# A scheduled attention and softplus kernel: the order of all tasks taken from a list of ranks, and the scheduler's durations reset

## The chip, the cores and the metric

The kernel runs on one core of a Trainium2 chip. The metric is the device time of one execution in microseconds (us); lower is better. A core has five engines that run side by side, each working through its own queue of instructions in order: PE (TensorE, matrix multiplication), ACT (ScalarE), DVE (VectorE), POOL (GpSimd) and SP (SyncE, which here only issues DMA transfers). They wait for each other through semaphores.

## The reference

```python
# q, k, v: (8, 8, 576, 64) float32 = batch, heads, rows, head size
kv  = einsum('bhsd,bhse->bhde', k, v)
out = einsum('bhsd,bhde->bhse', q, kv)
rms = sqrt(mean(out * out, axis=-1, keepdims=True) + 1e-06)
x   = (out / rms * g_norm), as (4608, 512)        # batch*rows, heads*head size
h   = x @ w_in                                    # w_in  (512, 2048), float64
g   = maximum(h, 0) + log1p(exp(-abs(h)))         # softplus
result = g @ w_out                                # w_out (2048, 512), float64
```

## The kernel before

**Arithmetic.** Each float32 operand of the large products is split into three parts, so that every product is a sum of three matmuls in a fast float32 format. The parts are made by ACT (`high`, and the copies that scale) and by DVE (`low`, `less`). The weights come as 64-bit floats: DVE and ACT take them apart with some eight instructions for each 128 x 512 piece (`weight`, lines 423 to 464) and split them (`split_weight`, lines 499 to 529).

**Stages.** There are 36 tiles of 128 rows.
- Attention: `kv_of` multiplies k and v of a batch (PE line 696), `rows` makes one tile of x: `turn_q` (PE line 776), `out_rows` (PE line 720), square (ACT line 793), sum (DVE line 724), root (POOL lines 727 and 728), norm (DVE line 732), `turn_x` (PE line 738).
- Narrow steps, `step`: 64 of them, over 12 blocks of 384 rows and the first four to six of 16 pieces of the hidden width. A step is `mm1` (PE line 864, 12 matmuls of 384 columns), softplus and split (ACT lines 886 and 888, DVE lines 875 and 879), and three `mm2` (PE line 871, three matmuls of 512 columns each). `mm1` of a block's first step needs the split of all three tiles of its block (`split`, ACT line 640, DVE lines 643 and 646).
- Wide steps, `wide_step`: 48 of them, over blocks of 512 rows and pairs of pieces. Each has seven products of six matmuls of 256 columns (PE line 1066, a scheme that saves one product in eight), copies of partial sums in between (ACT lines 1108 and 1112, DVE line 1116), softplus and split, and eight `mm2` of three matmuls of 512 columns (PE line 1137).

**Who sets the order.** No loop does. The code makes some 3,800 tasks with `plan.add`: the engine, an estimate of its time in ns, a function that issues the instructions, the tasks it needs, a place `pos` in a rough order, and the buffers that it takes and gives back. `Plan.order` then plays the program through: it keeps for each engine the time at which it is free, takes the tasks that could begin within `SOON` = 150 ns of the earliest one, and among those the one with the lowest `pos`. At the end the tasks are issued in the order of their planned starts. So durations, landing times and `pos` decide nothing but the order of each engine's queue; what the chip then does is up to the semaphores. In the kernel before, `pos` comes from formulas with some 150 numbers (`P0` to `P7`).

**Fillers.** Where the plan sees the tensor engine idle for 400 ns or more before the seventh `mm1`, it puts in a multiplication of unit matrices whose result nobody reads (`warm`, PE line 1232). Once in the queue it is executed, whether the engine is idle there or not.

**Loads.** All on SP's queue, in the order of the plan. A load that has a `behind` is also held until a certain `mm1` is done.

Of the kernel before, what the change touches and what calls it, by code (L numbers as in the profile page):

```python
# [18 lines left out]
P = 128  # L19
# [4 lines left out]
E = 1.0 / RADIX  # L24

# [35 lines left out]
class Plan:  # L61
# [4 lines left out]
    HANDOVER = {"PE": 250, "ACT": 120, "DVE": 120, "POOL": 150, "SP": 0}  # L66
    READY = {"PE": 2500, "ACT": 2500, "DVE": 4000, "POOL": 2500, "SP": 700}
    SWITCH = {("all", "rows"): 90, ("all", "kv"): 90, ("rows", "all"): 250, ("kv", "all"): 250, ("rows", "kv"): 140, ("kv", "rows"): 140}
    TOGETHER, PATIENCE = 1, 0.0
    LANDING, FILLED = 3500, 60000  # L70
# [13 lines left out]
    def add(self, engine, ns, run, after=(), pos=0.0, take=(), give=(), size=0, behind=None, follows=None, kind="all"):  # L84
        pos, behind = round(pos, 4), None if behind is None else round(behind, 4)
        t = Task(engine, ns, run, [a for a in after if a is not None], pos, list(take), list(give), size)
        for s in t.give:
            s.readers += 1
        self.tasks.append(t)
        t.follows = follows  # L90
        t.behind = behind
        t.kind = kind
        return t

    def order(self):
# [5 lines left out]
        ready = {}  # L101
# [24 lines left out]
        dma_free = 1500  # L126
        last_read = {}
        kind = "all"
        done, left = [], len(self.tasks)
        while left:  # L130
            best = None
            for engine, tasks in ready.items():
                options = []
                for t in tasks:
                    at = max(engine_free[engine], t.ready)
                    if t.size:
                        at = max(at, dma_free - 2500)
                    for i, s in enumerate(t.take):
                        others = sum(u.ring == s.ring for u in t.take[:i])
                        if engine == "SP" and s.ring in ("m", "n"):  # L140
                            others += self.KEEP
                        if len(free[s.ring]) <= others:
                            break
                        at = max(at, sorted(free[s.ring])[sum(u.ring == s.ring for u in t.take[:i])][0])
                    else:
                        options.append((at, t))
                if not options:
                    continue
                first = min(at for at, _ in options)
                options = [(at, t) for at, t in options if at <= first + self.SOON]  # L150
                small = [o for o in options if engine == "PE" and o[1].kind != "all"]
                if small:
                    rest = [o for o in options if o[1].kind == "all"]
                    if kind != "all":
                        options = [o for o in small if o[1].kind == kind] or small
                    elif rest and len(small) < self.TOGETHER and (
                            min(o[1].pos for o in small) + self.PATIENCE > min(o[1].pos for o in rest)):
                        options = rest
                at, t = min(options, key=lambda o: (o[1].pos, o[0]))
                if engine == "PE" and self.spare and self.spare[-1].start is None:  # L160
                    ring, run, ns, _ = self.spare
                    begin = max(engine_free["PE"], self.BEGIN, min(free[ring])[0] if free[ring] else at)
                    if begin + ns <= at:
                        s = Slot(ring)
                        at, t = begin, Task("PE", ns, lambda s=s: run(s), [], None, [s], [s], 0)
                        t.kind = "all"
                        s.readers = 1
                if best is None or at < best[0]:
                    best = (at, t)
            if best is None:  # L170
                raise RuntimeError("the plan is stuck at " + str([(e, t.pos, [s.ring for s in t.take if not free[s.ring]]) for e, ts in ready.items() for t in ts][:20]))
            at, t = best
# [9 lines left out]
            if t.engine == "PE":  # L182
                t.ns += self.SWITCH.get((kind, t.kind), 0)
                kind = t.kind
            t.start = at
            engine_free[t.engine] = at + t.ns
            t.end = at + t.ns + self.HANDOVER[t.engine]
            if t.size:
                dma_free = max(dma_free, at + t.ns) + t.size
                t.end = dma_free + (self.LANDING if dma_free > self.FILLED else 2000)  # L190
# [16 lines left out]
def kernel(  # L207
# [206 lines left out]
    def weight(j, pos, fetch_pos, behind):  # L414
# [11 lines left out]
        f = add("SP", 450, fetch, (), fetch_pos, [raw], size=1800, behind=behind)  # L426
        if wide:
# [43 lines left out]
            over_done.append(add("ACT", 910, beyond, [d3], pos + (4 if c < 4 else 0), [], [sq]))  # L471
# [136 lines left out]
    def load_q(b):  # L608
# [13 lines left out]
        for a in range(4):  # L622
            for p in range(0, NP, 2):
                q_loads[b].append(add("SP", 500, lambda a=a, p=p: run(a, p), (), pos + 0.1 * (2 * a + p // 2),
                                      [q_slots[b]] if not (a or p) else [], [], 1095, behind=pos - 3.5,
                                      follows=q_loads[b][-1] if a or p else None))

    def split(t, x, ready, pos):
# [20 lines left out]
        a = add("ACT", 640, high, [ready] + ([] if i == 0 else [first_high[n]]), pos, [dst] if i == 0 else [])  # L649
# [17 lines left out]
    def kv_of(b):  # L667
# [7 lines left out]
        for p in range(NP + 1):  # L675
# [4 lines left out]
            def load(src, s, p=p, tail=tail, n=n, ks=ks):  # L680
                if tail:
# [6 lines left out]
                       650 if tail else 850, behind=pos - 5.5) for of_v, (src, s) in enumerate(((k, ks), (v, vs)))]  # L688
# [11 lines left out]
            last = add("PE", 470, run, lds + ([last] if b < 2 else []), pos + 0.5 * p, [bank] if p == 0 else [], [ks, vs], kind="kv",  # L700
# [3 lines left out]
        kv_ready[b] = [add("ACT", 400, lambda: nc.scalar.copy(kvs[b % 2], bank.tile), [last] + o_tasks.get(b - 2, []),  # L704
                           pos + 2.5, [], [bank])]

    def rows(t):
# [38 lines left out]
        for b, r0, n, s0 in parts(t):  # L746
# [32 lines left out]
            ld = add("SP", 900, load, (), pos - EARLY[7] + P7[20 + t], [q_s] if not at_qa or t == 0 else [], [], 1220 * n // P,  # L779
                     behind=pos - 3.5, follows=first_load[0] if t and at_qa else None)  # L780
            first_load.append(ld)
            a = add("PE", 440, turn_q, [ld], pos - 1, [tp], [q_s])
            turned.append(add("ACT", 590, lambda n=n, r0=r0, tp=tp: nc.scalar.copy(part_of_qT(n, r0), tp.tile[:, :, :n]),  # L783
# [5 lines left out]
        a = o_task = add("PE", 484, out_rows, turned + need, x_pos(t - second), [o], [qT], kind="rows", follows=rows_done.get(t - 1))  # L789
        rows_done[t] = a  # L790
        for pt in parts(t):
            o_tasks.setdefault(pt[0], []).append(a)
        a = add("ACT", 600, lambda: nc.scalar.activation(new(x, [P, H, D]).rearrange("s (a k) d -> s a (k d)", k=2), o.tile, func=AF.Square,
                                                              scale=D ** -0.5), [a], pos, [x])
        a = add("DVE", 690, reduce, [a], pos, [r])
        a = add("POOL", 2300, root, [a], pos)
        a = add("DVE", 700, norm, [a, o_task], pos, [], [o, r])
        if t < BY_PE:
            a = add("PE", 440, turn_x, [a], pos + 0.5, [xp], [x])
            if t < AT_ONCE:  # L800
                split(t, xp, a, pos + 0.5)
            a = add("ACT", 600, lambda: nc.scalar.copy(new(xg, [P, KD, P]), xp.tile), [a], pos + 1, [xg], [xp])
            x_there[t] = [add("SP", 450, lambda: nc.sync.dma_start(
                out=x_of(t), in_=xg.tile), [a], pos + 1, [], [xg], 1000)]
            return
# [21 lines left out]
        if i == g - 1:  # L827
            stores = [add("SP", 450, lambda a=a: store(a), turns, pos + 0.5, [], [xb], 820 if g > 1 else 490)
                      for a in range(P // BL)]
            for u in range(t - i, t + 1):  # L830
                x_there[u] = stores
# [6 lines left out]
    def x_again(t):  # L838
# [3 lines left out]
                 x_there[t], pos - EARLY[9], [xt], [], 1000, behind=first_step["block", t // TB] - 5)  # L842
# [6 lines left out]
    def step(s):  # L849
# [32 lines left out]
        a = add("PE", 2100, mm1, x_split[n] + factors_done[0, c] + [m for _, m in mm1s[-1:]] +  # L882
# [9 lines left out]
        for i in range(TB):  # L892
            a2 = add("PE", 700, lambda i=i: mm2(i), [a] + factors_done[1, c] + [mm2s.get(i)], s + 1.5,
# [19 lines left out]
    def leave(ph, t, bank, done, pos):  # L913
# [20 lines left out]
        if ph == LAST and BY_PE <= t < n_tiles - TB:  # L934
# [8 lines left out]
            add("SP", 1600, store, [a], pos, [], [ot], 750)  # L943
# [15 lines left out]
    def units_of(ph, n):  # L959
# [3 lines left out]
        for j, us in enumerate(GROUPS):  # L963
# [9 lines left out]
            def fetch(v, src, after, size, first=first, xl=xl, x_part=x_part, pos=pos, cols=None):  # L973
# [3 lines left out]
                t = add("SP", 350, run, after, pos - AHEAD, [] if first else [xl], [], size, behind=pos - 2 * AHEAD,  # L977
# [57 lines left out]
            a = add("ACT", 1070 if m > 1 else 600, high, lds, pos, [dst])  # L1035
# [8 lines left out]
    def wide_step(k):  # L1044
# [25 lines left out]
        def multiply(u, q, after, pos, take=(), follows=None):  # L1070
# [4 lines left out]
            return add("PE", 710, lambda: product(u, q), unit_done[ph, n, u] + forms_done[p][f] + list(after), pos, take, give,  # L1075
# [32 lines left out]
        c1 = add("ACT", 380, lambda: nc.scalar.copy(place(Y), place(X)), [a1, a5], b + 0.1)  # L1108
        c5 = add("ACT", 390, v_copy, [a5], b + 0.12, [gv])
        a6 = multiply(3, Y, [c1], b + LATE[0])  # L1110
        a2 = multiply(2, X, [c1, c5], b + LATE[0] + 0.02, follows=a6)
        c6 = add("ACT", 380, lambda: nc.scalar.copy(place(Z), place(Y)), [a6], b + 0.65)  # L1112
        x2 = add("ACT", 400, lambda: softplus(gt()[:, 0, :HW], place(X)), [a2], b + 0.7)
# [7 lines left out]
        x4 = add("ACT", 400, lambda: softplus(gt()[:, 1, :HW], place(Z)), [a4], b + 1.9, [], [ab])  # L1121
# [39 lines left out]
        for c in range(2):  # L1161
            for i in range(TW):
                slot_pos = b + PACE + MM2[TW * c + i]
                a2 = add("PE", 700, lambda c=c, i=i: mm2(c, i),
# [70 lines left out]
    plan.spare = ("h", warm, 400, mm1s[6][1])  # L1235
    for t in plan.order():
        t.run()
# [30 lines left out]
```

## Time and profile before

| | |
|---|---|
| median of 3 runs | 858.6 us (857.62 to 860.17) |
| the profiled execution | 858.19 us, of which the span from the first to the last instruction is 856.4 us |
| PE busy | 843.0 us, 98% of the span |
| DVE busy | 704.1 us, 82% |
| ACT busy | 520.6 us, 61% |
| POOL busy | 76.6 us, 9% |
| moved by DMA | 167.07 MB, mean 195 GB/s |

Busy time of PE is counted from a matmul's start to its modelled end, so consecutive matmuls overlap in it; how long one task holds the engine is read from start to start. The first `mm1` starts at 44.09 us, the narrow steps reach to about 355 us, and the last matmul ends at about 852.6 us.

### The profile page before, as it was taken

Reading aid. Unit: us, or ns where it says so; the run is one execution under the profiler, and the core shown is the slowest. Engines: PE = TensorE matmul, PEld = TensorE weight load, DVE = VectorE, ACT = ScalarE, POOL = GpSimd, SP = SyncE. Lnnn points to the kernel's source line nnn. Section 1 sums busy time; section 2 is a strip of 40 time slices with the busy share of each in tenths; the row PEclk is TensorE's granted clock in tenths of the full one; section 3 lists DMA queues with packets and bytes.
Section 4 is the critical chain, followed back from the end, with each engine's and each line's share of the span. In section 5 each row is a group of like instructions: output and inputs, shape, how many; then the busy total and the mean of one; then the engine's idle time right before and its main releaser. Section 6 shows DMA issues by size and latency. Waiting matters only on the chain.

```text
span 856.4 us, 17075 instructions
## 1 busy us (share of the span) xinstructions
PE 843.0 (98%) x6464; PEld 754.1 (88%) x6464; DVE 704.1 (82%) x995; ACT 520.6 (61%) x980; POOL 76.6 (9%) x79
## 2 busy tenths in 40 slices
PE   8899999999999999999999999999999999999998
PEld 5578898999898999999999999998999899999996
DVE  7888898888788889798898788878788766788873
ACT  6766665446344567766667665655868555566654
POOL 0351223111113300000000000000000000000000
PEclk9999999999999999999999999999999999999999
DMA  9998997778884755436644546645364753777864
GB/s 283 297 233 212 261 273 232 185 245 218 214 188 119 194 160 185 142 110 207 210 156 154 180 151 206 195 158 181 124 197 138 234 168 102 240 237 246 249 189 131
DMA packets 239778, 167.07 MB, mean 195 GB/s; under 512 B 106320, under 2 KB 198736, under 8 KB 239696
## 3 DMA queue, kind: packets, MB, share of 16 engines
q1 hardware_dynamic: 239392, 165.86, 65.9%
q8 instruction: 50, 0.82, 0.4%
q14 instruction: 32, 0.26, 0.1%
q10 hardware_dynamic: 304, 0.13, 0.1%
HBM read 112.98 MB, written 52.95 MB: 194 GB/s over the span
## 4 chain that ended last, share of the span: by engine, by line
PE 94%; ACT 1%; DVE 1%; DMA 1%; issue 1%; POOL 0%; SPq 0%; POOLq 0%; DVEq 0%; ACTq 0%
PE banks L1137 31%; PE banks L1066 28%; PE banks L871 16%; PE banks L864 15%; PE banks L720 2%; PE banks L696 2%; DMA loads<-in_k_dram 1%; PE banks L738 0%; PE banks L1232 0%; PE banks L776 0%; DVE units L643 0%; DVE half L732 0%; DVE roots L724 0%; POOL roots L728 0%; ACT w L783 0%
## 5 line engine op out<-in xcount | busy, mean ns | idle before, releaser
L1137 PE MATMUL banks<-pieces,gv 128*128 128x512 f32 x768 | 236.8, 390 | 0.0
L1137 PE MATMUL banks<-pieces,g_False 128*128 128x512 f32 x384 | 149.4, 389 | 0.0
L1137 PEld LDWEIGHTS banks<-pieces,gv 128*128 128x128 f32 x768 | 132.5, 188 | 17.2 <-DVE banks L910 0.2
L864 PE MATMUL banks<-units,pieces 128*128 128x384 f32 x768 | 144.8, 337 | 0.0
L871 PE MATMUL banks<-pieces,gv 128*128 128x512 f32 x576 | 143.3, 393 | 0.0
L864 PEld LDWEIGHTS banks<-units,pieces 128*128 128x128 f32 x768 | 134.7, 188 | 4.5
L871 PEld LDWEIGHTS banks<-pieces,gv 128*128 128x128 f32 x576 | 106.2, 188 | 19.0
L1066 PEld LDWEIGHTS banks<-units,pieces 128*128 128x128 f32 x840 | 111.0, 188 | 6.5 <-ACT banks L1112 0.4
L1066 PE MATMUL banks<-units,pieces 128*128 128x256 f32 x840 | 115.2, 280 | 0.0
L886 ACT ACTIVATE half<-banks 128x384 f32<-128x384 f32 x64 | 31.4, 491 | 94.0 <-PE banks L864 90.7
L1127 DVE TENSOR_TENSOR gv<-g_True,gv 128x1024 fp32r<-128x1024 f32 x47 | 57.5, 1223 | 35.6 <-ACT gv L1124 35.5
L1137 PEld LDWEIGHTS banks<-pieces,g_False 128*128 128x128 f32 x384 | 72.1, 188 | 15.0
L1066 PEld LDWEIGHTS banks<-units,w 128*128 128x128 f32 x504 | 66.7, 188 | 3.7 <-ACT banks L1112 0.2
L1066 PE MATMUL banks<-units,w 128*128 128x256 f32 x504 | 69.6, 280 | 0.0
L728 POOL TENSOR_TENSOR roots<-roots,half 128x8 f32<-128x8 f32 x36 | 62.3, 1731 | 3.0
L1130 DVE SCALAR_TENSOR_TENSOR g_False<-gv 128x1024 fp32r<-128x1024 f32 x47 | 57.6, 1225 | 1.5
L1029 DVE TENSOR_TENSOR units<-loads,units 128x1024 fp32r<-128x1024 f32 x42 | 51.2, 1219 | 6.0 <-ACT units L1026 5.9
L1094 ACT ACTIVATE g_True<-banks 128x256 f32<-128x256 f32 x96 | 36.7, 384 | 30.6 <-PE banks L1066 29.9
L1116 DVE TENSOR_TENSOR g_True<-banks,g_True 128x512 f32<-128x512 f32 x48 | 33.1, 690 | 25.8 <-PE banks L1066 19.8
L931 ACT ACTIVATE m<-banks 128x512 f32<-128x512 f32 x72 | 42.1, 595 | 18.2 <-PE banks L1137 12.5
L1032 DVE SCALAR_TENSOR_TENSOR units<-units 128x1024 fp32r<-128x1024 f32 x42 | 51.4, 1224 | 1.7
L1026 ACT ACTIVATE units<-loads 128x1024 fp32r<-128x1024 f32 x42 | 44.3, 1056 | 12.4 <-PE banks L1066 10.1
(115 smaller groups left out, 1248.7 us busy)
## 6 DMA issues: line engine op xcount, KB each, us to landing
loads<-x SPq DMA_DIRECT2D x180, 128.0 KB, 2.7
part<-m SPq DMA_DIRECT2D x72, 256.0 KB, 3.1
m<-part SPq DMA_DIRECT2D x72, 256.0 KB, 3.4
loads<-form SPq DMA_DIRECT2D x45, 256.0 KB, 3.2
form<-loads SPq DMA_DIRECT2D x36, 256.0 KB, 3.0
raw<-in_moe_w_in_dram SPq DMA_DIRECT2D x16, 512.0 KB, 4.7
loads<-in_k_dram SPq DMA_DIRECT2D x32, 256.0 KB, 4.0
loads<-in_v_dram SPq DMA_DIRECT2D x32, 256.0 KB, 4.5
```

The costliest lines, as they stand in the source:

```text
L728: nc.gpsimd.tensor_tensor(out=r.tile, in0=r.tile, in1=half, op=ALU.pow)
L864: nc.tensor.matmul(from_the_end(hp, w), lhsT=w_in.tile[:, i, kd * P:(kd + 1) * P], rhs=from_the_end(xv.tile[:, i, kd], w), start=(m == 0), ...
L871: nc.tensor.matmul(mine[i].tile, lhsT=gv.tile[:, m, i * P:(i + 1) * P], rhs=w_out.tile[:, m], start=(c == cs[0] and m == 0), stop=(c == cs ...
L931: a = add("ACT", 690 if ph == LAST else 600, lambda: nc.scalar.activation(new(ot, [P, d_model]), bank.tile, func=AF.Copy, scale=scale if p ...
L1026: nc.scalar.activation(part_of(0, F32R), xl.tile if m > 1 else xl.tile[:, 0], func=AF.Copy, scale=DOWN)
L1029: nc.vector.tensor_tensor(out=part_of(1, F32R), in0=xl.tile if m > 1 else xl.tile[:, 0], in1=part_of(0), op=ALU.subtract)
L1032: nc.vector.scalar_tensor_tensor(out=part_of(2, F32R), in0=part_of(1), scalar=-RADIX, in1=part_of(0), op0=ALU.mult, op1=ALU.add)
L1066: nc.tensor.matmul(from_the_end(place(q), (16, 8)[kd]), lhsT=w[:, m, at:at + P], rhs=from_the_end(dst.tile[:, m, v, kd] if u < 6 else dst. ...
L1094: nc.scalar.activation(dst, src, func=AF.Softplus, scale=1.0 + E)
L1127: nc.vector.tensor_tensor(out=gvt(1, F32R), in0=gt(), in1=gvt(0), op=ALU.subtract)
L1130: nc.vector.scalar_tensor_tensor(out=gt(F32R), in0=gvt(1), scalar=-RADIX, in1=gvt(0), op0=ALU.mult, op1=ALU.add)
L1137: nc.tensor.matmul(from_the_end(mine[i].tile, P), lhsT=(gvt(m, F32R) if m < 2 else gt(F32R))[:, c, i * P:(i + 1) * P], rhs=from_the_end(ou ...
```

## The change

Three things change; no task is added, taken away or altered.

1. The scheduler's estimates: tasks of ACT, DVE and POOL are taken shorter by a constant (`AHEAD`), hand-over times and several durations are reset, a change of the kind of matmul is priced differently, a load is priced by an entry time, its size and a fixed landing, and holds back later ones when too many descriptors or transfers are under way (`room`). Tasks on the PSUM rings `o` and `tp` wait until other engines have left the ring (`touched`).
2. After all tasks are made, each `pos` is overwritten by a number of the list `RANK`.
3. `Plan.order` runs as before with these, and lays in its fillers by its own reading.

```diff
+RANK = [
+    0, 7, 8, 9, 10, 12, 13, 14, 19, 22, 24, 28, 33, 38, 1, 16, 17, 21, 27, 30, 31, 34, 37, 42, 47, 51, 55, 61, 18, 44, 43, 45, 49, 53, 54, 57, 60, 64, 79,
...
+    3779, 3781, 3783, 3782, 3785, 3788, 3784, 3787, 3790, 3789, 3791, 3792, 3793, 3794,
+]
...
-    HANDOVER = {"PE": 250, "ACT": 120, "DVE": 120, "POOL": 150, "SP": 0}
-    READY = {"PE": 2500, "ACT": 2500, "DVE": 4000, "POOL": 2500, "SP": 700}
+    HANDOVER = {"PE": 205, "ACT": 140, "DVE": 121, "POOL": 145, "SP": 0}
+    AHEAD = {"PE": 0, "ACT": 107, "DVE": 88, "POOL": 110, "SP": 0}
+    READY = {"PE": 1600, "ACT": 3250, "DVE": 3050, "POOL": 2500, "SP": 700}
...
-    LANDING, FILLED = 3500, 60000
+    ENTRY, LANDING, DESCS, MOVES = 1770, 790, 2560, 8
...
-        t = Task(engine, ns, run, [a for a in after if a is not None], pos, list(take), list(give), size)
+        t = Task(engine, ns - self.AHEAD[engine], run, [a for a in after if a is not None], pos, list(take), list(give), size)
...
-                    at = max(engine_free[engine], t.ready)
-                    if t.size:
-                        at = max(at, dma_free - 2500)
+                    at = max([engine_free[engine], t.ready, *(end for b in t.banks for e, end in touched[b].items() if e != engine)])
...
+            if t.size:
+                at = room(t, at)
...
-                dma_free = max(dma_free, at + t.ns) + t.size
-                t.end = dma_free + (self.LANDING if dma_free > self.FILLED else 2000)
+                dma_free = max(dma_free, at + self.ENTRY) + t.size
+                t.end = dma_free + self.LANDING
...
-            return add("PE", 710, lambda: product(u, q), unit_done[ph, n, u] + forms_done[p][f] + list(after), pos, take, give,
+            return add("PE", 700, lambda: product(u, q), unit_done[ph, n, u] + forms_done[p][f] + list(after), pos, take, give,
...
+    assert len(RANK) == len(plan.tasks)
+    for t, at in zip(plan.tasks, RANK):
+        t.pos = at
     for t in plan.order():
         t.run()
```

`RANK` has 3,795 numbers, one for each task in the order in which the code makes them, and no number twice. Sorted by it, every task stands behind all that it needs, so the list can be read as one order of the whole program. For PE, up to the ninth `mm1`, with one letter for a task (M `mm1`, 2 `mm2`, k `kv_of`, r `out_rows`, q `turn_q`, x `turn_x`, l the two matmuls of a weight's split; fillers left out):

```
before      kkqlqlkkkqlrrqqkxlqqkrrxkqlxkkqrxrMxrlqxMkkrMxrl2x22222xM22kkk2rrMl22kkr2xMx222M222M222x22M
by RANK     qqlkkqlqqkkklrrlqqkkrxlqxrklkkxrrxMlMxM2rkkq2q22r22xMkkkr2xx2l2rM2M2xrkk2rM22M22x22x222M
```

## The prediction, made before the changed kernel was run

> **What bounds the kernel now.** I began with the windows view, which sets the engines side by side stage by stage.
>
> ```profile
> core 0: us, PE busy (x) PEld busy (x) DVE busy (x) ACT busy (x) POOL busy (x), PEclk, DMA share, GB/s
> 4.70:44.00 39.30, 32.72 (x458) 23.43 (x457) 35.33 (x60) 30.13 (x60) 9.55 (x11) 1.00 1.06 299
> 44.00:64.00 20.00, 18.68 (x214) 15.54 (x213) 17.35 (x31) 12.70 (x25) 9.80 (x9) 1.00 0.93 237
> 64.00:94.00 30.00, 29.89 (x306) 25.76 (x305) 26.40 (x46) 19.80 (x40) 6.44 (x6) 1.00 0.90 230
> 355.30:856.40 501.10, 497.33 (x3162) 450.96 (x3160) 399.11 (x470) 313.48 (x574) 0.00 (x0) 1.00 0.58 182
> ```
>
> From 64 us on PE has no gap to speak of; before that it has, while DVE is busy 90% of the time and the DMA engines all of it. So only the start can give much. What PE does there is seen in the groups by line and in the timeline:
>
> ```profile
> L1232 PE MATMUL banks<-ident_r 128*128 128x512 f32 x52 | 18.8, 480 | 2.0 <-DVE ident_r L1192 1.6 <-ACT pieces L529 0.2
> ```
>
> ```profile
> 42.59 1.66 PE L1232 MATMUL banks<-ident_r 128*128 128x512 f32 x6
> 44.09 2.25 PE L864 MATMUL banks<-units,pieces 128*128 128x384 f32 x12
> ```
>
> L1232 is the filler: 52 of them, 50 of these before the first `mm1` starts at 44.09 us. A busy PE is therefore not a useful PE, and I counted useful time instead. From start to start in the timeline, a task that follows its own kind takes: `mm1` 2.086 us, `mm2` 0.680, a product 0.700, a wide `mm2` 0.680. So 64 x 2.086 + 192 x 0.68 + 336 x 0.70 + 384 x 0.68 = 760.4 us; the small tasks (40 `kv_of` of 0.468, 36 `out_rows` of 0.515, 22 transposing tasks of about 0.38, 8 of 0.55 and a few more) add 50.7. Useful work W = 811.1 us of a span of 856.4: **45.3 us are lost**. With x the useful work that is done by a moment t, the loss so far is t - x:
>
> - first `mm1`: t 44.1, x 15.5, lost 28.6
> - fourth `mm1`: t 63.9, x 31.7, lost 32.2
> - ninth `mm1`: t 93.7, x 59.2, lost 34.5
> - end of the narrow steps: lost 40.5; wide steps: about 1 more; behind the last matmul, while the last tile is stored: 3.9.
>
> The ninth `mm1` opens the third block. Its DVE split ends at 92.9 us, 0.8 us before it starts, and the thirteenth likewise: DVE's queue sets the openings of blocks, up to about 115 us.
>
> **The change part by part.** No instruction is added, so W stays. I read `RANK` as an order (every task stands behind its needs), put in the durations above, and compared what stands ahead of what. Fillers, and swaps within 150 ns, I can't read from it.
>
> *To the first `mm1`.* 34 PE tasks ahead in both; on DVE 64 tasks ahead, before 62. Back to back, two DVE instructions of 0.69 us start 0.61 us apart (34.21 and 34.82 us), so +1.2 at most. Against it: the six fillers ahead of the first `mm1`, 1.5 us, may not stand there. I take 0; bounds -1.5 and +1.2.
>
> *First to ninth `mm1`.* In the new order the second and third `mm1` follow the first with one small task in between each (x 18.3 and 20.7, before 19.8 and 23.3). The last DVE instruction that the first `mm2` needs has 8 fewer DVE tasks ahead of it (70, before 78), 4.9 us. Splits of later tiles move back in exchange. The ninth `mm1` has the same DVE work ahead (73.1 us by the kernel's estimates less 88 ns each, before 73.4) but less useful PE work behind it: x 57.5, before 59.2. If DVE gets there no sooner, that is a loss of 1.7 - 0.3 = +1.4. But DVE idles: 39.3 - 35.33 + 20 - 17.35 + 30 - 26.40 = 10.2 us of the 89 before that point. The waits view says for what (ACT's squares, roots, PE's rows): neighbours in the queue that were not ready. That is what a better order takes away. With none of it regained +1.4; with all of it -8.8, but the changes of kind on PE (an `mm1` ahead of a `kv_of` takes 2.18 us instead of 2.09) can't go, about 1.6 of the 5.9 lost here, so -4.3 at the most. I take half, 1.4 - 5.1 = **-3.7**: the named waits of DVE from 44 to 116 us add to 6.9 us, so about half of the idle time belongs to neighbours that another order can exchange, and the rest to chains in which one DVE instruction feeds the next.
>
> *Rest of the narrow steps.* 6.0 us are lost here. In the whole order PE changes 75 times between `kv_of`, `out_rows` and the rest, before 70: 5 x 0.09 = +0.5. Between an `mm1` and the first `mm2` that needs it, beyond ACT's and DVE's time, lies a median of 7.2 us of PE work, before 3.0. That cushion covers waits of the kind that PE has at 77.5 us, where an `mm2` of 0.68 us holds it for 0.95. I take -1.1 for them, so **-0.6**; bounds -2 and +1.5.
>
> *Wide steps.* In the order before, 4 places have one product only between a product and the next that needs ACT's copy of it, 0.06 us more than copy and hand-overs take; PE lost 0.00, 0.07, 0.09 and 0.11 us at them. In the new order there are 27, and 5 wide `mm2` stand 0.1 us too early for their split. So 23 x 0.07 + 5 x 0.1 = +2.1; less the 1 us that the old stalls cost, which fall where the order is now another: **+1.1**; bounds -0.5 and, with 0.11 and late copies at each, +4.
>
> *Loads.* Their distance to their use, in PE work:
>
> ```profile
> DMA to landing us min/median/max: 2.1/2.8/5.2
> ```
>
> That is line 976, the wide steps' loads of x. The shortest PE work between such a load and the product it feeds, less ACT's and DVE's time, falls from 7.6 to 4.7 us; for the 72 loads of partial sums (median 3.4, longest 6.1) it stays 4.1. At the median nothing waits: 0, bounds 0 and +2, in the range. [...]
>
> *End.* The last `mm2` run is the same 15 tasks: 0.
>
> Sum: 0 - 3.7 - 0.6 + 1.1 + 0 = -3.2. The profiled execution took 858.19 us (1.8 around the span), 0.4 under the median of 858.6; so 855.0, or **855.4** for a median.
>
> **The rivals.**
> 1. *DVE's queue is as slow as before.* Then the ninth `mm1` comes at +1.4 and the sum is 0 + 1.4 - 0.6 + 1.1 = +1.9, with +1.2 ahead of the first `mm1` and +1.5 for the narrow steps +5.2: 860.5, up to 863.8. It ends slower, in DVE's queue ahead of the ninth and thirteenth `mm1`, and it decides from the point where DVE regains less than 1.4 us of idle time. For it: ahead of the fifth `mm1`, which opens block two, the new order has 55.5 us of DVE work, before 43.1. Against it: idle time with named waits is there to be had.
> 2. *The gain is given back in the wide steps.* All 27 tight places cost 0.11, loads land late, ACT's queue stands wrong: +4 there, so 858.6 - 3.7 - 0.6 + 4 = 858.3. For it: PE has no gap there now, so any disorder can only cost. Against it: some 28 old places with 0.44 us to spare cost nothing.
> 3. *DVE regains nearly all of it.* -4.3 - 1.5 - 2 + 0 = -7.8: 850.8.
> 4. *The clock falls.* The first 13 fillers start 0.43 us apart up to 6.9 us, later ones 0.23: PE ran at half speed there, though the row of the granted clock shows 1.00. If the new fillers leave a longer gap near 45 us, two `mm1` at half speed cost 2 x 2.09 = 4.2: 859.6. [...]
>
> That the change does nothing can be left out: of 1,085 PE tasks only 177 keep the same successor.
>
> **How the numbers follow.** Forecast 0.45, rivals in order 0.22, 0.18, 0.10, 0.05. The forecast's own range is 851 to 858. A measurement of this kernel can tell about 0.3%, 2.6 us: faster is under 856.0, slower over 861.2. Faster: 0.36 of the forecast and all of rival 3, 0.46. Within: 0.09 of the forecast, 0.05 of rival 1, 0.11 of rival 2, 0.02 of rival 4, 0.27. Slower: 0.17 of rival 1, 0.07 of rival 2, 0.03 of rival 4, 0.27. The range runs from rival 3's 850.5 to 863, close to rival 1's end.
>
> **What would show it.** Right: the first `mm1` within 1.5 us of 44.1; the fourth at a loss of about 30 (t near 60); the ninth before 90 us; DVE busy over 92% from 44 to 90; fewer than 45 fillers; the wide stage 0 to 2 us longer. Wrong: the ninth `mm1` at 92 us or later, a PE row in the waits view above 1 us past 100 us, or a wide stage over 4 us longer.

## The result, and the profile after

The changed kernel takes 865.52 us (median of six runs, 864.3 to 868.38) where the kernel before took 858.73 beside it: a ratio of 1.0086, 95% interval 1.0066 to 1.0106. It is slower by 6.8 us; the forecast was 3.2 us faster. The profiled execution took 865.74 us, its span is 864.0 (before 856.4).

The windows view of the changed kernel, over nearly the stretches that were shown of before (columns: stretch, length, then busy time and instructions of PE, PEld, DVE, ACT and POOL, granted clock, share of the DMA engines, GB/s):

```profile
4.70:44.00 39.30, 30.27 (x378) 21.87 (x376) 33.63 (x58) 28.66 (x57) 9.21 (x9) 0.87 0.98 271
44.00:64.00 20.00, 19.67 (x248) 16.61 (x247) 18.56 (x33) 12.85 (x27) 6.57 (x7) 1.00 0.98 246
64.00:94.00 30.00, 29.18 (x334) 25.26 (x333) 25.92 (x45) 21.17 (x43) 11.35 (x10) 1.00 0.99 259
356.00:864.00 508.00, 504.19 (x3177) 453.81 (x3175) 397.26 (x470) 311.91 (x575) 0.00 (x0) 1.00 0.57 180
```

Between 44 and 64 us DVE is indeed busier than before (18.56 us, was 17.35). But the first row has a granted clock of 0.87 where before had 1.00, and from 64 to 94 us PE is now the less busy one. The filler and the first `mm1`, in the groups by line and the timeline, and the loads of x in the view of their line:

```profile
L1401 PE MATMUL banks<-ident_r 128*128 128x512 f32 x42 | 15.4, 482 | 1.6 <-DVE ident_r L1361 1.6
```

```profile
46.73 2.36 PE L1033 MATMUL banks<-units,pieces 128*128 128x384 f32 x12
```

```profile
DMA to landing us min/median/max: 2.1/2.8/5.8
```

Ten fillers fewer, the first `mm1` 2.6 us later, and loads that land as before, at the median. (Lines of the changed kernel stand 169 further down: L864 is L1033, L1066 is L1235, L1112 is L1281.)

Where the 7.6 us of span went is seen with the prediction's own measure: t - x, the time that has passed less the useful PE work done by then. Each row is worked out from the starts of PE's tasks in one kernel's trace; the kernels below the second row are the experiments that follow.

| lost at x = | 0 | 15.6 (first `mm1`) | 30 | 60 | 110 | 320 | 810 |
|---|---|---|---|---|---|---|---|
| before | 8.4 | 28.6 | 32.2 | 34.5 | 36.9 | 40.6 | 41.6 |
| changed | 9.9 | 31.1 | 32.7 | 35.7 | 40.4 | 44.2 | 49.2 |
| clock_kept | 9.7 | 29.6 | 31.2 | 34.4 | 38.2 | 41.9 | 47.9 |
| wide_old_own | 9.8 | 28.7 | 30.3 | 34.7 | 39.3 | 42.7 | 43.6 |
| wide_new_own | 8.9 | 31.5 | 35.1 | 37.4 | 39.8 | 45.9 | 51.0 |
| after_short | 9.7 | 30.2 | 31.9 | 35.9 | 39.7 | 43.1 | 46.7 |
| before_short | 8.5 | 30.5 | 34.1 | 36.4 | 38.9 | 42.6 | 43.3 |
| after_split | 9.5 | 29.1 | 30.7 | 34.9 | 39.4 | 42.7 | 53.2 |
| before_split | 8.2 | 29.6 | 33.2 | 35.5 | 38.0 | 41.6 | 43.7 |
| start_new | 9.6 | 30.5 | 32.1 | 43.6 | 46.1 | 49.8 | 50.7 |
| start_old_own | 8.5 | 28.7 | 35.9 | 39.2 | 43.0 | 47.4 | 52.4 |
| narrow_new | 9.7 | 29.6 | 31.2 | 33.7 | 37.0 | 40.6 | 41.8 |
| narrow_new_clock | 9.6 | 27.4 | 29.0 | 31.8 | 35.5 | 39.2 | 40.2 |
| margin | 9.3 | 31.4 | 33.8 | 36.1 | 39.5 | 45.7 | 48.6 |
| margin_old_start | 8.4 | 28.1 | 31.0 | 33.3 | 37.7 | 43.3 | 44.7 |

Row by row, the changed kernel loses 2.4 us more than before up to the first `mm1`, wins 2.0 from there to x = 30 (the fourth `mm1`), and loses 0.8 to x = 60, 2.2 to x = 110, 0.2 to the end of the narrow steps and 3.9 in the wide steps: together the 7.6, but for rounding.

Two stretches can be read across kernels that have the same order there. From x = 15.6 to x = 30 the changed order loses 1.6 to 1.7 us and the old one 3.6, in every one of them. The first column that counts, x = 15.6, is not so sure: with the changed start and no added fillers it is 28.7 to 31.1, with the old start 28.1 to 31.5. So one execution differs from the next by some 3 us there, and most of the 2.4 us between the first two rows may be chance: over the six rows with each start the mean is 29.9 for the changed one and 29.5 for the old.

### The profile page after: what moved, and what is told of

Read it like the earlier page. It is cut to its first block, busy times and chain, and to the rows that moved or that the text cites. A ratio compares the mean times of both kernels' runs of the same rounds, so it can differ in the third digit from the quotient of the medians.

```text
span 864.0 us, 17031 instructions
## 1 busy us (share of the span) xinstructions
PE 847.4 (98%) x6454; PEld 753.9 (87%) x6454; DVE 697.6 (81%) x995; ACT 518.4 (60%) x980; POOL 79.2 (9%) x79
## 4 chain that ended last, share of the span: by engine, by line
PE 94%; DMA 3%; ACT 1%; DVE 1%; SPq 0%; issue 0%; DVEq 0%; ACTq 0%
PE banks L1306 30%; PE banks L1235 28%; PE banks L1040 15%; PE banks L1033 14%; PE banks L865 2%; PE banks L889 2%; DMA loads<-in_k_dram 1%; DMA early<-in_q_dram 1%; DMA raw<-in_moe_w_in_dram 1%; PE banks L1401 1%; PE banks L907 0%; PE banks L945 0%; DMA g<-in_k_dram 0%; SPq L854 0%; PE banks L694 0%
## 5 line engine op out<-in xcount | busy, mean ns | idle before, releaser
L1306 PE MATMUL banks<-pieces,gv 128*128 128x512 f32 x696 | 215.3, 391 | 0.0
L1040 PE MATMUL banks<-pieces,gv 128*128 128x512 f32 x576 | 147.8, 395 | 0.2 <-DVE gv L1048 0.2
L1033 PE MATMUL banks<-units,pieces 128*128 128x384 f32 x768 | 145.2, 337 | 0.1
L1033 PEld LDWEIGHTS banks<-units,pieces 128*128 128x128 f32 x768 | 134.6, 188 | 5.2 <-ACT half L1055 0.6
L1306 PE MATMUL banks<-pieces,g_False 128*128 128x512 f32 x348 | 135.6, 390 | 0.0
L1306 PEld LDWEIGHTS banks<-pieces,gv 128*128 128x128 f32 x696 | 119.6, 188 | 15.3
L1235 PEld LDWEIGHTS banks<-units,pieces 128*128 128x128 f32 x924 | 121.0, 188 | 8.5 <-ACT banks L1281 2.3
L1235 PE MATMUL banks<-units,pieces 128*128 128x256 f32 x924 | 127.6, 282 | 0.0
L1040 PEld LDWEIGHTS banks<-pieces,gv 128*128 128x128 f32 x576 | 105.3, 188 | 18.5 <-DVE gv L1048 0.7
L1306 PEld LDWEIGHTS banks<-pieces,g_False 128*128 128x128 f32 x348 | 65.3, 188 | 13.9
L1263 ACT ACTIVATE g_True<-banks 128x256 f32<-128x256 f32 x96 | 36.3, 379 | 42.6 <-PE banks L1235 41.9
L1235 PE MATMUL banks<-units,w 128*128 128x256 f32 x384 | 54.2, 281 | 0.0
L1235 PEld LDWEIGHTS banks<-units,w 128*128 128x128 f32 x384 | 51.3, 188 | 3.1 <-ACT g_True L1260 0.2
L1195 ACT ACTIVATE units<-loads 128x1024 fp32r<-128x1024 f32 x41 | 43.3, 1057 | 16.5 <-PE banks L1235 9.9
L1293 ACT ACTIVATE gv<-g_True 128x1024 fp32r<-128x1024 f32 x47 | 49.9, 1061 | 1.4
```

What stands on the lines that cost most here:

```text
L1033: nc.tensor.matmul(from_the_end(hp, w), lhsT=w_in.tile[:, i, kd * P:(kd + 1) * P], rhs=from_the_end(xv.tile[:, i, kd], w), start=(m == 0), ...
L1040: nc.tensor.matmul(mine[i].tile, lhsT=gv.tile[:, m, i * P:(i + 1) * P], rhs=w_out.tile[:, m], start=(c == cs[0] and m == 0), stop=(c == cs ...
L1195: nc.scalar.activation(part_of(0, F32R), xl.tile if m > 1 else xl.tile[:, 0], func=AF.Copy, scale=DOWN)
L1235: nc.tensor.matmul(from_the_end(place(q), (16, 8)[kd]), lhsT=w[:, m, at:at + P], rhs=from_the_end(dst.tile[:, m, v, kd] if u < 6 else dst. ...
L1293: nc.scalar.activation(gvt(0, F32R), gt(), func=AF.Copy, scale=DOWN)
L1306: nc.tensor.matmul(from_the_end(mine[i].tile, P), lhsT=(gvt(m, F32R) if m < 2 else gt(F32R))[:, c, i * P:(i + 1) * P], rhs=from_the_end(ou ...
```

## The experiments

Most of these kernels keep all instructions and change queues. Their edit is the same few lines: `Plan.order` no longer chooses, it follows a list of tasks (-1 is a filler) and a list of the buffers that each task had in the order it comes from. Each ratio is to the kernel before, run again beside that kernel (medians 858.4 to 859.8).

```diff
-        while left:
-            best = None
...
+        for item in ORD:
+            t = self.tasks[item]
...
+                for f in free[s.ring]:
+                    if n < len(wanted) and f[1] == wanted[n]:
+                        place = f
```

**Which stage.** The old order behind the changed narrow steps, and the changed order behind the old ones. In the first pair about 250 tasks got other buffers than in the order they come from, in the second pair, "own", only about ten.

> All engines' queues follow the new order up to the last narrow step (the first 1,620 of the 3,837 entries) and the old order from there on. Theory A (the wide steps lose 3.9 us in the new order because products stand too close to the copies they wait for): 865.5 - 3.9 = 861.6 us, PE from 356 us on as in the kernel before. Theory B (loads that come late and a cold start are the whole loss, the wide steps only pass it on): 864.5 to 865.5 us.

> The opposite: the old order up to the last narrow step, the new order for the wide steps. Theory A: 858.7 + 3.9 = 862.6 us, with some 37 stalls of 30 to 110 ns of PE behind 356 us. Theory B: 858.7 to 859.5 us.

> As wide_old (new order up to the last narrow step, old order from there), but each task takes the buffer that it had in the order it comes from, but for 12 tasks; in wide_old 252 tasks had another. Theory A (the order of the wide steps costs 3.9 us): the wide steps lose 1.0 us as in the kernel before, 865.5 - 3.9 = 861.6 us. Theory E (which buffer is taken counts as much as the order): wide_old's 863.2 us falls by the 1.4 us that its wide steps lost over those of before, to 861.8 us; if buffers do not count it stays at 863.2.

> As wide_new (old order up to the last narrow step, new order from there), with each task's own buffer but for 8 tasks; in wide_new 233 had another and the wide steps lost 10.8 us. Theory A: 858.9 + 3.9 = 862.8 us. Theory E: the same, and 5 us below wide_new's 867.9. If buffers do not count: 867.9 again.

Measured: 863.17 (ratio 1.0043, 1.0029 to 1.0057) and 867.92 (1.0100, 1.0085 to 1.0115); with their own buffers 859.60 (1.0015, 1.0004 to 1.0025) and 865.96 (1.0079, 1.0065 to 1.0093). Taking the changed wide order away brings back 5.9 of 6.8 us (by the two intervals, give or take some 2 us); putting it behind the old narrow steps costs 7.3, of which some 2.4 arise at the seam (6.1 us lost from x = 110 to 320, in before 3.7). Which buffer a task gets matters as well: 863.17 or 859.60 with one and the same order.

**The start.** Nine more fillers ahead of PE's first task, and nothing else changed; then the old order for the first 260 or 270 entries with the changed order behind it.

> The changed kernel with 9 more fillers ahead of the first task of PE, so that PE does not stand still from 6.05 to 9.90 us. Theory C (PE's half speed from 9.9 to 17.3 us delays the k and v products, these hold the four load buffers, and the loads start late): first mm1 at 45 us or before, 865.5 - 1.5 = 864.0 us or less. Theory D (the start is late because of the order of the loads alone): first mm1 at 46.5 us, 865.3 us or more.

> The old order up to the first mm1 (its first 260 entries, fillers included), the new order from there. Theory A': the first mm1 is back at 44.1 us instead of 46.7, and the narrow steps keep the whole of it: 865.5 - 2.4 = 863.1 us. Theory B': DVE's queue takes most of it back by the ninth mm1, as it did in the changed kernel (loss there 35.7, before 34.5): 864.5 to 865.5 us.

> Old order up to just behind the first mm1 (270 entries), new order from there, each task with its own buffer but for 6 tasks; in start_old 516 had another, and it took 875.2 us. Theory A' (the late start is kept to the end): 865.5 - 2.0 = 863.5 us. Theory B' (DVE's queue takes it back by the ninth mm1): 865 us. If buffers do not count: 875 us.

clock_kept took 863.41 (1.0051, 1.0039 to 1.0063), 2.1 us under the changed kernel; the same fillers were worth 1.9 us in each of two other orders further down. The timeline of PE in the changed kernel and the windows view of both, changed kernel first, show why:

```profile
3.90 2.15 PE L1401 MATMUL banks<-ident_r 128*128 128x512 f32 x7
9.90 1.09 PE L945 MATMUL banks<-ident_r,early 128*128 128x128 f32 x4 [3.85 <-DMA early<-in_q_dram]
...
12.77 0.78 PE L694 MATMUL banks<-pieces,ident_r 128*128 128x512 f32 x1
...
17.31 0.40 PE L694 MATMUL banks<-pieces,ident_r 128*128 128x512 f32 x1
```

```profile
0.00:10.00 10.00, 4.55 (x13) 3.36 (x14) 6.04 (x15) 3.92 (x6) 0.93 (x7) 0.91 0.78 229
10.00:20.00 10.00, 9.86 (x66) 7.08 (x66) 8.92 (x16) 7.88 (x17) 0.00 (x0) 0.75 0.92 245
20.00:30.00 10.00, 7.41 (x127) 5.50 (x127) 6.96 (x13) 6.15 (x13) 0.00 (x0) 0.83 0.98 287
```

```profile
0.00:10.00 10.00, 7.55 (x24) 5.83 (x25) 5.96 (x15) 3.85 (x6) 0.97 (x7) 1.00 0.79 230
10.00:20.00 10.00, 8.09 (x66) 5.14 (x65) 9.28 (x17) 8.45 (x18) 0.00 (x0) 1.00 1.07 311
20.00:30.00 10.00, 8.46 (x152) 6.24 (x152) 9.69 (x17) 9.05 (x19) 2.99 (x3) 1.00 1.09 317
```

PE stood still for 3.85 us behind its few fillers, and the same matmul then took 0.78 us at 12.8 us and 0.40 at 17.3. The granted clock is 0.50 from 9.9 to 14.9 us and 0.99 from there to 20, so the half speed lasts for 5 us of work and not to 17.3 us, as the expectation had it. With the fillers PE is kept running, the clock stays at 1.00 in these three stretches, and the DMA engines move 311 and 317 GB/s in the second and third stretch where they moved 245 and 287. The trace of the changed kernel has a second fall, to 0.83 between 20 and 30 us, where PE had waited only 1.7 and 0.8 us; in before, where PE's longest wait is 1.6 us, the clock is 1.00 in all three stretches. How long a wait brings the clock down is not shown.

The fall comes with this start more often than with the old one. In the first 30 us the granted clock is 0.83 to 0.94 in all eight profiled kernels that begin with the changed order and no added fillers, and 1.00 in all four that have the fillers. With the old start it is 1.00 in five of eight.

start_old took 875.23 (1.0190, 1.0166 to 1.0213) and start_old_own 869.07 (1.0119, 1.0103 to 1.0135): slower than either parent. The table shows why this says little of the start: up to the seam start_old_own is at 28.7, as before is, and within 3 us of useful work behind the seam it loses 4.8 more, where tasks of two different queues meet. Behind the waits there, of which the longest is 2.5 us, the granted clock falls too, to 0.83 between 50 and 60 us.

**The wide steps: turn-round behind one product.** My first try exchanged neighbours on PE alone so that only 9 of the 32 tight places stayed.

> The changed kernel with 74 places of PE's queue in the wide steps exchanged, so that 23 of the 32 products and mm2 that stand too close to a copy or a split get one more PE task in between; all other queues and all buffers as they are. Theory A (tight places, each some 0.06 us and as much again in the tasks behind it): 865.5 - 23 x 0.13 = 862.5 us, stalls of PE over 25 ns behind 356 us fall from 37 to some 14. Theory F (the stalls come from ACT's queue or from late loads, wherever the product stands): 865 us, stalls as many as before.

It took 875.63 (1.0190, 1.0174 to 1.0205), 10 us more than the changed kernel, and the waits view of its weight loads begins with other waits than copies (the two copies have 1.8 us):

```profile
PEld banks L1351 <- ACT g_True L1376: 8.4, 11, 1.5
PEld banks L1422 <- DVE banks L1195: 2.6, 2, 1.4
```

I read this so: the queues of ACT and DVE were those of the old neighbours, and moving one queue alone made worse places than it mended. So I left every queue as it was and changed the length of the suspected step itself: the two ACT copies between products, first cut to half their columns, then made in two halves.

```diff
-lambda: nc.scalar.copy(place(Y), place(X))
+lambda: nc.scalar.copy(place(Y)[:, :P], place(X)[:, :P])                # short
...
+def halfway(a, b):                                                       # split
+    nc.scalar.copy(place(a)[:, :P], place(b)[:, :P])
+    nc.scalar.copy(place(a)[:, P:], place(b)[:, P:])
```

> The changed kernel, but the two ScalarE copies between products of a wide step (rows L1277 and L1281, 95 of them, 362 ns each) copy 128 of their 256 columns; the sums of the other columns are left wrong. ScalarE's rows of 256 and 512 columns (379 and 630 ns) give about 1 ns a column, so each copy should take about 0.13 us less. Theory (turn-round): the changed order has 27 places where only one 0.70 us product stands between a product and the one that needs its copy (4 in the kernel before), and product, copy and next product take 0.03 to 0.11 us longer than that; 20 of the 37 stalls in the wide steps are of this kind. Then the shorter copy takes away 15 to 25 of the 37 stalls, the wide steps lose 2 to 3 us and not 4.9, and the time is 862.3 to 863.7 where the changed kernel took 865.5. Rival (the stalls come from PE's own order, its weight loads, or from a ScalarE that is busy with other work then): 30 or more stalls stay and the time is 865 to 866.

> The kernel before with the same two copies cut to 128 columns. Theory (turn-round): it has 4 such places and 6 stalls in its wide steps, so it gains 0 to 0.5 us (858.2 to 858.7). Rival (ScalarE as a whole bounds the wide steps): it gains as the changed kernel does, 1 us or more.

> The changed kernel with each of the two ScalarE copies between products of a wide step made as two copies of 128 columns. One of 256 columns took 362 ns and one of 128 took 256, so a pair should take 0.10 to 0.15 us longer. Theory (the changed order has no slack there): 27 places with one product between, each later by that, and the products behind them: 2.5 to 5 us, so 868 to 870.5. Rival (only the longest waits matter, the queue takes up the rest): within 1 us of 865.5.

> The kernel before with the same copies made in two halves. Theory (slack): only 4 such places, so 0.2 to 0.8 us: 859 to 859.7. Rival (ScalarE's time itself counts in the wide steps): 2 us or more, as much as the changed kernel.

| | time | ratio to before | stalls over 25 ns in the wide steps | lost in the wide steps |
|---|---|---|---|---|
| after_short | 863.26 | 1.0053 (1.0039 to 1.0066) | 16 | 3.6 |
| changed | 865.52 | 1.0086 (1.0066 to 1.0106) | 37 | 5.0 |
| after_split | 869.79 | 1.0130 (1.0117 to 1.0144) | 70 | 10.5 |
| before_short | 858.46 | 0.9996 (0.9987 to 1.0005) | 2 | 0.8 |
| before | 858.73 | 1 | 6 | 1.0 |
| before_split | 860.11 | 1.0011 (1.0001 to 1.0021) | 12 | 2.1 |

The times of after_short, before_short and after_split are those that the theory gave; before_split is over its 859 to 859.7. But the wide steps of after_short still lose 3.6 us and not 2 to 3: of the 2.3 us that it gains in time only 1.4 are seen there, and most of the rest lies ahead of the first `mm1`, where executions differ by more. So the two copies are shown to cause stalls. What the changed wide steps lose beyond the old ones with short copies (3.6 against 0.8) is not taken away by any run here.

The waits view of PE's weight loads in the wide steps, for the changed kernel, for before, for after_split and for before_split in turn (waiting line, what it waited for, us in all, times, longest):

```profile
PEld banks L1235 <- ACT banks L1281: 2.5, 12, 0.2
PEld banks L1235 <- ACT banks L1277: 1.5, 8, 0.2
PEld banks L1235 <- ACT g_True L1260: 0.6, 3, 0.2
```

```profile
PEld banks L1066 <- ACT banks L1112: 0.6, 3, 0.2
```

```profile
PEld banks L1235 <- ACT banks L1264: 8.6, 25, 0.4
```

```profile
PEld banks L1066 <- ACT banks L1095: 1.3, 4, 0.4
```

With the split copy the 27 tight places give 25 waits and the old order's 4 give 4; with the short copy the rows of L1277 and L1281 are gone from the list. One such place in the timeline of the changed kernel, when only one wide `mm2` stands between a product and the one that needs its copy:

```profile
728.43 0.86 PE L1235 MATMUL banks<-units,w 128*128 128x256 f32 x6
728.44 0.65 PEld L1235 LDWEIGHTS banks<-units,w 128*128 128x128 f32 x5
...
729.33 0.36 ACT L1277 COPY banks<-banks 128x256 f32<-128x256 f32 x1 [1.46 <-PE banks L1235]
...
729.74 0.78 PEld L1235 LDWEIGHTS banks<-units,w 128*128 128x128 f32 x6 [0.19 <-ACT banks L1277]
729.81 0.91 PE L1235 MATMUL banks<-units,w 128*128 128x256 f32 x6
```

ACT is idle until the product ends, the copy ends at 729.69, and only then, at 729.74, does the first weight load begin. In the undisturbed product at 728.43 five of six loads fall beside the matmuls, the first one, at 728.21, lay ahead of them; here all six come late. The tasks behind lose as well: the 37 stalls of the changed kernel are 2.1 us, the five or six tasks behind each, 10 to 20 ns longer apiece, another 2.0, and the rest 0.85. This second part does not grow with the stall. From start to start, the tasks that took 5 to 25 ns too long add up to 2.8 us in the changed kernel, 2.7 in after_short and 3.0 in after_split (before: 0.5), while the stalls over 25 ns add up to 2.1, 0.7 and 7.5 us. Behind a product that came only some 20 ns late in after_short the same tail is seen. So a late product costs its delay and, in the changed kernel, about 0.05 us more (2.0 us over 37), however short the delay was. That the late weight loads are what makes this tail is my reading of the one place above.

**Is the early gain kept?** The changed order to the fourth `mm1`, then the old one, without and with the fillers; and the same with the seam at the fifteenth `mm1`.

> The changed order to its 350th entry (just behind the fourth mm1), from there the order of before, buffers as each order had them but for 4 tasks. If what the new start wins (1.9 us at the fourth mm1, by the curve of lost time) is kept by the old order, which has slack in its queues: 856.4 to 858.0. Rival (from there on it is loads, VectorE and ScalarE, not PE's lead, that set the old order's pace, so it is given back before 100 us): 858.3 to 860.0. Second rival (a changed prefix does not fit, as where the new order followed the old start): 862 or more.

> As the kernel with the new start and the old order behind it, with nine more fillers ahead of PE's first task, which had brought the changed kernel 2.1 us. If the cold clock counts here too and the lead is kept: 855.5 to 857.5. If the lead is given back by 100 us: as the kernel without the fillers, within 1 us.

> The changed order to its 640th entry (behind the fifteenth mm1, 125 us), the old order from there, buffers as each order had them but for 6 tasks. The kernel's own scheduler, with the changed constants, replays the old order at 857.4 and this one at 855.4, and it replays both the same 3 to 4 us later when every handover is set 60 ns longer. If that replay holds for the old order's part and the gain at the fourth mm1 outlives the first 110 us: 856.4 to 857.6. Rival (the changed order gives its 1.9 us back between 65 and 125 us, as its curve of lost time has it): 858.5 to 860.

> As narrow_new, with nine more fillers ahead of PE's first task. If the low clock of the first 30 us takes part of the gain: 1 to 2 us below narrow_new, 855 to 857. If it does not count once the old order follows: within 0.5 us of narrow_new.

start_new took 867.89 (1.0103, 1.0089 to 1.0117) and start_new_clock 865.97 (1.0080, 1.0068 to 1.0093). Again it is the seam, 9.2 us of start_new's loss between x = 35 and 40, seen in its waits view from 60 to 85 us:

```profile
PE banks L1023 <- DVE half L1017: 5.5, 2, 3.2
```

Part of it is the clock: from 70 to 80 us, behind these waits, it is 0.50. Behind the seam the old order loses 7.4 us from x = 45 to the end, in before's own trace 7.5: it keeps what lead or lag it is given. narrow_new, whose seam costs nothing that can be seen, took 859.60 (1.0011, 1.0002 to 1.0021), the rival's case: from x = 15.6 to 30 it gains the 2 us (1.6 lost, before 3.6), and by x = 110 it stands where before does, at 37.0 and 36.9. narrow_new_clock took 857.75 (0.9992, 0.9983 to 1.0001). It is the best of all orders here, 1.9 us under the same order without the fillers, as start_new_clock is under start_new, and still not to be told from the kernel before.

**An order with margin.** The kernel's own scheduler, with the changed constants, can replay any order. It gives the old order 857.4 and the changed one 849.2. With longer hand-overs and landings the two change places, as the expectation below has it. So I searched orders myself, with a score that weighs three such replays.

> All instructions as before, order from a search of mine over the kernel's own replays with the changed constants, scored not by the plain replay alone but by 0.3 of it, 0.4 of one with handovers 60 ns and landings 500 ns later, and 0.3 of one with 120 and 1000 ns. It starts from narrow_new_clock and leaves its first 47 us alone. Replays: 848.5, 851.0, 855.8 (the changed order 849.2, 865.8, 902.8; the old one 857.4, 864.4, 877.9). Theory (the changed order failed for want of slack): the narrow steps end 2.4 us sooner than in the replay of the old order, the wide steps lose no more than 1 us, so 854 to 857. Rival (any order searched on this replay loses on the chip what the replay promises, since the replay is wrong otherwise): 862 to 867.

> The same search with the same score, started from the old order and leaving its first 45 us alone. Replays: 849.2, 852.1, 856.9; the narrow steps end 1.7 us sooner than in the old order's replay. Theory (slack): 855 to 858, and no more than 10 stalls in the wide steps. Rival (the replay is no guide): 862 or more.

Measured: 863.93 (1.0043, 1.0028 to 1.0057) and 862.91 (1.0041, 1.0029 to 1.0053). My expectation fell, and the rival's number came. (The search knew only the needs that the scheduler lists and could exchange steps that only a queue had kept apart, so in both orders part of the sums is wrong; instructions and sizes are the same.) It was half right for the wide steps: 14 and 8 stalls and 2.9 and 1.4 us lost there, against 37 and 5.0. But the narrow steps, from the first `mm1` to x = 320, lose 14.3 and 15.2 us, where before loses 12.0 and the changed kernel 13.1.

## Why the prediction was wrong

Its four terms, with what was measured in the two profiled executions:

- *To the first `mm1`: 0 (-1.5 to +1.2).* Measured +2.4 in these two, outside; but the means of the table's rows are 29.9 and 29.5, so +0.4, inside, and most of the 2.4 is the spread of the start. What the term left out all the same is the clock, worth 2.1 us to the changed kernel by clock_kept. The mechanism is rival 4's, but at 6 to 15 us (3.85 us of waiting, then a granted clock of 0.50), not at 45: I had noted that fillers might not stand where they stood and looked only at those just ahead of the first `mm1`, not at those ahead of PE's first task.
- *First to ninth `mm1`: -3.7 (+1.4 to -4.3).* Measured: 31.1 to 35.7 lost, before 28.6 to 34.5, so -1.3. The mechanism was right in its first half: ahead of 48.3, 51.9, 57.1 and 59.6 us PE had lost 2.4 us in before (start to start; the timeline shows 1.3 of it as idle), and none of these waits is left. "Half of DVE's idle time regained" was the size that failed. From 44 to 90 us DVE, the third pair of numbers, is busy 40.37 us in before and 41.19 us in the changed kernel:

```profile
44.00:90.00 46.00, 44.57 (x497) 37.94 (x496) 40.37 (x71) 29.26 (x59) 16.24 (x15) 1.00 0.91 230
```

```profile
44.00:90.00 46.00, 44.85 (x560) 38.52 (x559) 41.19 (x72) 32.06 (x65) 15.36 (x15) 1.00 0.98 253
```

That is 0.8 us regained in this stretch, not 5.1. The half was also badly founded: the 10.2 us of idle time were counted from 4.7 to 94 us, the 6.9 us of named waits from 44 to 116.

- *Rest of the narrow steps: -0.6 (-2 to +1.5).* Measured +2.4, outside. Between x = 60 and 110 the changed order has 24 changes of kind between `kv_of`, `out_rows`, transposes and the rest, before 15, at some 0.1 us each (in before an `mm1` takes 2.18 us ahead of a `kv_of` at 96.44 us, and 2.09 ahead of an `mm2` at 83.57); I had the count of the whole order, 75 against 70, and took the cushion of PE work to outweigh it. And PE waits 0.95 us at 133 us (a `kv_of`, 0.8 of it for a load of k) and 0.52 at 219, as no task of before does there.
- *Wide steps: +1.1 (-0.5 to +4).* Measured +3.9, the largest term. The count was right: 27 and 5 places were foreseen, and 25 waits show when the copy is lengthened. The stalls themselves also came out at the 2.1 us of the sum, in part by luck, for by the waits view only 20 of the 37 wait for one of the two copies. What it put at nothing is what the tasks behind a late product lose, another 2.0 us; 0.85 us came in small losses elsewhere.

*Loads* and *end* were 0 as forecast: PE's waits view names no load in the wide steps, and 3.8 us lie behind the last matmul in both. The +2 at the upper end of *loads* is shown by no run: the wide steps' loads of x landed after 2.8 us at the median and 5.8 at the longest, before 2.8 and 5.2. ACT and DVE did wait longer for the loads of x, 8.5 us where before had 2.8; what that cost PE was not tried.

Two executions are a poor measure of the parts, so the medians should be read beside them. The changed start and narrow steps with the old wide steps (wide_old_own) are 0.9 us slower than before, where the first three terms promised 4.3 us faster; the changed wide steps make the other 5.9 us, where the fourth term had 1.1. (The two profiled executions of the changed wide order with untouched copies and its own narrow steps lose 5.0 and 6.0 us there.) So two steps failed: DVE's idle time was not regained, and the wide steps were priced too low.

Of the rivals, the second came true in its place (+4 in the wide steps), the fourth in its mechanism, and the first in its verdict and its sign: DVE regained 0.8 us, under the 1.4 it set, and the ninth `mm1` came at 93.2 us, where 92 was to be the sign. What none of them had is that these come together. I added up terms as if each could go its own way, and in the two profiles all but the early gain came out at its bad end or beyond. The scheduler's replay suggests that this is no accident. Against the chip's span:

| order | the scheduler's replay | span on the chip |
|---|---|---|
| before | 857.4 | 856.4 |
| narrow_new_clock | 855.4 | 854.9 |
| start_new | 864.1 | 865.5 |
| wide_old_own | 855.3 | 858.4 |
| wide_new_own | 853.2 | 865.8 |
| changed | 849.2 | 864.0 |
| margin | 848.5 | 863.4 |
| margin_old_start | 849.2 | 859.5 |

The old order, which was not found on this replay, comes out within 1 us of the chip. Orders that were searched on it, or that have searched wide steps, come out 10 to 15 us too good; the searched narrow steps alone, in wide_old_own, 3. I take from this that a search finds the order in which the replay's errors help most: a copy set to arrive in the very 0.7 us that it takes is one of them, and that such a place costs time on the chip was shown. The two orders searched with margin lose less in the wide steps, but in all they are still 14.9 and 10.3 us too good. What the replay has wrong in the narrow steps is open. More changes of kind (37 and 34 behind x = 110, before 27) and single waits of 1 to 1.3 us are seen there, but I tried nothing that takes them away.

## What to carry to other kernels

An order that is searched on a model must be judged by what it was not searched on: the same model on the old order, and both with every hand-over and landing a little later, before any run. If the new order's lead melts there, distrust it; if it holds, that is no proof, for margin's held (851.0 against 864.4 in its expectation) and margin was slower on the chip. Where a planned wait has no slack, count the stall and a charge for the tasks behind it, here some 0.05 us however short the stall; and don't add such terms as if they were independent. Look at the clock ahead of the first real work as well as at the queue: nine fillers there were worth 1.9 to 2.1 us in three orders. To test a suspected tight step, change its length and leave the queues alone: a hybrid of two orders measures its seam first.

## What the runs showed of the hardware

- In the changed kernel, after 3.85 us without work, PE ran at half rate for 5 us of nearly unbroken work (granted clock 0.50 from 9.9 to 14.9 us), and the clock fell again between 20 and 30 us (0.83), where the waits ahead were 1.7 and 0.8 us.
- The same first entries of a queue bring the first `mm1` at losses of 28.7 to 31.1 us in different executions, so two starts can't be compared by one profile of each kernel.
- Half the columns of a 128 x 256 copy take 256 of its 362 ns, and two halves 0.14 us more than the whole. after_split, which has the halves at all 27 tight places, lost 5.5 us more in its wide steps than the changed kernel.
- The buffer that a task is given moved the time of one order from 859.60 (1.0015, 1.0004 to 1.0025) to 863.17 (1.0043, 1.0029 to 1.0057): wide_old_own and wide_old. Why was not looked into.
